# A Fourier mixing layer followed by a low-rank and channel mixer: late loads folded by quarters, u summed in PSUM, and a split last store

## The chip, the cores and the metric

The kernel runs on one core of a Trainium2 chip. The core has TensorE (PE, matmuls into PSUM; PEld is its weight load), VectorE (DVE), ScalarE (ACT), GpSimd (POOL) and SyncE (SP, which here only starts DMAs). Each has a queue of its own that it works off in order, and they wait for one another by semaphores. The metric is the device time of one execution in microseconds; of several executions the median is given.

## The reference

For each of 8 batches, `x` is a matrix of 3136 rows (sequence) and 256 columns. The first layer takes the real part of a two-dimensional Fourier transform. The second adds a low-rank mix along the sequence and then a two-layer channel mix with a residual:

```python
X = np.fft.fft(np.fft.fft(x, axis=1), axis=2).real
h = X.transpose(0, 2, 1) @ U @ V          # U: 3136 x 32, V: 32 x 3136
u = X + h.transpose(0, 2, 1)
out = u + np.maximum(u @ w_ch1, 0.0) @ w_ch2   # 256 -> 1024 -> 256
```

## The kernel before

**Transform.** The real part of the transform is symmetric, so only half of the rows (1568 per batch) is computed directly and the others are obtained as mirror images. Rows of `x` are loaded in four quarters q = 0..3, in two tiles: `xf` by GpSimd's gathers (`load_f`, line 69, one quarter each) and `xr` by SP's plain DMAs (`load_r`, line 74, one or two quarters each). "EV" is the quarters 0 and 2, "OD" 1 and 3. VectorE folds them: `along_d` (line 415) subtracts or adds columns and their mirror images into the bf16 tiles `EOF_` and `EOR_`; `alone` (line 422, on GpSimd) copies the two columns that have no partner; `mirror` (430) folds two quarters into `EOS`; `half` and `fourth` (434, 443) make `GE`, `GO` and `GC` of that. TensorE then multiplies these with tables of sines and cosines that ScalarE made at the start (`seq` at 539, `even_rows` at 595). ScalarE copies the first half of each product into `ev`, VectorE forms `eh` (`apart`) and joins the parts into the tiles `A` and `B` (`join`, `mirrored`). A second, short transform along the channels, `chan` (650) and, for the first rows of batch 0, `first_rows` (683), multiplies `A` and `B` with `MC` and `MSN` (or `MSX`) and leaves S and T, the two halves of the 256 channels for all 1568 rows. Calls of `filler` issue matmuls whose results are not used.

**Mixer.** The 8 x 1568 rows are worked off in 25 chunks of 512 columns, the last of 256. `front` (738) makes u of a chunk: TensorE multiplies V by the low-rank table `TA`, and VectorE adds S or T to it. It is done once for the rows themselves (hf = 0) and once for their mirrors (hf = 1). `direct` (798) is the first channel product for hf = 0, with ReLU on ScalarE; `mirrors` (814) corrects the same PSUM banks with WD and `uo`, which is S minus T, for hf = 1. `second_product` (855) is the second channel product. For most chunks u is also transposed by a DMA into `ut`, and VectorE adds that to the product (lines 882, 883), GpSimd adding a correction to one or two columns (887). For chunk 0 there is no `ut`: TensorE adds u by a matmul with a unit matrix `EM`, and ScalarE copies the sum (878). `store` (848) sends the output of a chunk to memory.

**Order.** Up to line 1131 the order of each engine's queue is the order of the source lines, written out by hand; from there on a planner orders the steps, with matmuls and folds kept in program order, and `put` and `turn` spread the work for the next batch over the chunks by due times. In the part written by hand stand, in this order: the loads; the sine tables; the folds of OD of `xr` and EV of `xf`, then those of EV of `xr` and OD of `xf` (lines 982 to 1010); on GpSimd between them the loads of V, W1 and W2 (992 to 995), the first gathers of batch 1 (1000) and the memsets of one row of `MSN` (1002); a copy of it to `MSX` on ScalarE (1021); the products of batch 0 (1026 to 1060); `lowrank`, which makes `TA`; `first_rows(0, 0)`, `hidden_0` and `front(0, 0)`; then `direct(0, 0)` and `chan(0, 2, ...)`.

PSUM banks are handed out in turn by tag: "dft" has two, "p1" four, "p2" two.

Of the kernel before, what the change touches and what calls it, by code (L numbers as in the profile page):

```python
# [16 lines left out]
P = 128  # L17
# [14 lines left out]
def kernel(  # L32
# [105 lines left out]
    load_r(x, xr, 0, 1, 2, D)  # L138
    r3()
    f0()  # L140
    load_r(x, xr, 0, 0, 2, D)
    iota(jv[:], [[1, KP]], 0, 1)
    for q in (0, 2):
        load_f(x, xf, 0, q, D)
# [277 lines left out]
    def alone(qs, src, dst, eng=None):  # L422

        (eng or nc.gpsimd.tensor_copy)(dst[:, qs, :, 128:257:128], src[:, qs, :, 0:129:128])
# [258 lines left out]
    def first_rows(b, at, tag):  # L683

        d = ST[b]
        n = 256 if at == 0 else 136
        for h in range(2):
            pt = psum.tile([P, 2, 256], FP32, tag=tag, name="psf", bufs=BUFS[tag])
            for c, lo in enumerate((at, 785 + at)):
                mm(pt[:, c, :n], MC[:, h * P:(h + 1) * P], d["A"][:, lo:lo + n], start=True, stop=False)  # L690
                mm(pt[:, c, :n], MSN[:, h * P:(h + 1) * P], d["B"][:, lo:lo + n], start=False, stop=True)
            to = strip(d["ST"[h]][:], 2 * at, [[1, 2], [2, n]])
            if h == 1:
                nc.vector.tensor_copy(to, pt[:, :, :n])
            else:
                nc.scalar.copy(to, pt[:, :, :n])

    def transposed(b, spare):

# [145 lines left out]

    out_f = out.rearrange("b n d -> (b n) d")

    def store(c, hf):

        o = CK[c]["o", hf]  # L850
        for row, p, np_, t, nt in blocks(c, hf):
            nc.sync.dma_start(out=bass.AP(out.tensor, out.offset + row * D, [[D, np_], [P * D, nt], [1, D]]),
                              in_=o[p:p + np_, t:t + nt, :])

    def second_product(c, hf, t0, w=2, rows=P, between=None):

        k = CK[c]
        h, ut = k["h", hf], k.get(("ut", hf))
        if t0 == 0:
            k["o", hf] = cp.tile([P, CH // P, D], FP32, tag="o", name="o", bufs=2)  # L860
        p2 = psum.tile([P, 2, D], FP32, tag="p2", name="p2", bufs=2)
        o = k["o", hf][:rows]
        for t in range(w):
            if t and between:
                between()
            at = (t0 + t) * P
            for j in range(JT):
                mm(p2[:rows, t, :], h[j // 4][:, j % 4, at:at + rows], W2[:, j, :],
                   start=(j == 0), stop=(j == JT - 1))
            if ut is None:  # L870
                parts = ((0, 1, P + 1), (1, P + 1, D), (1, 0, 1)) if hf else ((0, 0, P), (1, P, D))
                for s_, lo, hi in parts:
                    src = EM[:, P:P + 1] if hi == 1 else EM[:, lo:hi]
                    mm(p2[:rows, t, lo:hi], k["u", hf][:, s_, at:at + rows], src,
                       start=False, stop=True, skip_group_check=True)
        ts = slice(t0, t0 + w)
        if ut is None:
            nc.scalar.copy(o[:, ts, :], p2[:rows, :w, :])
            return
        tT = slice(CH // P + t0, CH // P + t0 + w)  # L880
        p2 = p2[:rows]
        nc.vector.tensor_tensor(o[:, ts, 0:P], p2[:, :w, 0:P], ut[:rows, ts, 0:P], op=AL.add)  # L882
        nc.vector.tensor_tensor(o[:, ts, P:D], p2[:, :w, P:D],  # L883
                                strip(ut[:rows], (CH // P + t0 + 1) * P, [[P, w], [-1, P]]), op=AL.add)
        fx = k["fx", hf]
        cols = slice(0, P + 1, P) if hf else slice(P, P + 1)
        nc.gpsimd.tensor_tensor(o[:, ts, cols], o[:, ts, cols], fx[:rows, ts, 1 - hf:], op=AL.add)  # L887
# [100 lines left out]
    msr = MSN[0:1].rearrange("p (l two) -> p l two", two=2)  # L988
    MDT = [MSN, MC]

    alone(EV, xf, EOF_)
    nc.gpsimd.dma_start(out=VV[:R, 0:S], in_=moe_V)
    gather(w1t[:], moe_w_ch1, D, pint[:], H, 0)
    nc.gpsimd.dma_start(out=W1[:, 0, :], in_=moe_w_ch1[0:P, :])
    nc.gpsimd.dma_start(out=W2[:], in_=moe_w_ch2.rearrange("(j p) d -> p j d", p=P))
    alone(EV, xr, EOR_)
    alone(OD, xf, EOF_)
    for part in range(2):
        along_d(EV, xf, EOF_, part)
    for q in (0, 2):  # L1000
# [3 lines left out]
    mirror(0, slice(0, 128), AL.subtract)  # L1004
    mirror(0, slice(128, 258), AL.add)
    for part in range(2):
        along_d(EV, xr, EOR_, part)
    along_d(OD, xf, EOF_, 0)
    mirror(1, slice(0, 128), AL.subtract)
    mirror(1, slice(256, 258), AL.add)  # L1010
    fill = filler()
# [10 lines left out]
    msr = MSX[0:1].rearrange("p (l two) -> p l two", two=2)  # L1022
    nc.gpsimd.memset(msr[:, :, 0:1], -1.0)
    nc.gpsimd.memset(msr[:, :, 1:2], 1.0)
    fill(22)
    for cols in (slice(0, 128), slice(256, 258)):
        half(0, 1, cols)
    seq(0, 1, 0, 0, "dft", False)
# [35 lines left out]
    filler("p2", spare)(3)  # L1064
    transposed(0, spare)
    join(0, 1, 0, sin_odd, low=False)
    nc.vector.tensor_tensor(WD[:], W1[:, 1, :], W1[:, 0, :], op=AL.subtract)
# [12 lines left out]
    nc.vector.tensor_copy(VV[2 * R:, S:S + 1], VV[2 * R:, HALF:HALF + 1])  # L1080
# [54 lines left out]
    for c in range(1, NCH):  # L1135
# [16 lines left out]
        if c + 1 < NCH:  # L1152
# [39 lines left out]
```

## Time and profile before

| what | value |
|---|---|
| median of 3 executions | 445.69 us (445.62 to 453.18) |
| profiled execution | 445.72 us |
| its span | 443.9 us |
| TensorE busy | 426.4 us (96%), granted clock 0.999 |
| VectorE busy | 318.2 us (72%) |
| ScalarE busy | 292.2 us (66%) |
| GpSimd busy | 134.7 us (30%) |
| moved by DMA | 67.83 MB, 153 GB/s in the mean |

The span runs from the first to the last instruction that the profile records; the execution's own time contains it and a little before and after. Busy time counts what an engine executes, not what its queue spends on waiting. A row of an engine in order of time gives the start, the duration, the engine, the line, the operation with what it writes and reads, its shape and, in brackets, how long the engine sat idle before it and what ended that wait. Neighbouring instructions of one kind are merged (x8), and a pipelined instruction's duration can overlap the next one's start.

### The profile page before, as it was taken

How to read it: one execution, taken by the hardware profiler on the slowest of the kernel's cores; microseconds unless marked ns; L12 is line 12 of the kernel's file. 1: busy time of each engine (PE TensorE's matmuls, PEld its weight loads, DVE VectorE, ACT ScalarE, POOL GpSimd, SP SyncE). 2: the span in 40 equal slices, each digit the busy share in tenths (PEclk: the TensorE clock that was granted, in tenths of full speed). 3: DMA queues.
4: the chain of work that ended last, by engine and by line, in shares of the span. 5: the costliest groups of instructions: out<-in, count | busy, mean ns of one | idle time of the engine just before them, and what ended most of it. 6: DMA issues, size and time to landing. Idle time of an engine off the chain costs nothing.

```text
span 443.9 us, 9378 instructions
## 1 busy us (share of the span) xinstructions
PE 426.4 (96%) x3501; PEld 283.5 (64%) x3501; DVE 318.2 (72%) x660; ACT 292.2 (66%) x633; POOL 134.7 (30%) x338
## 2 busy tenths in 40 slices
PE   5999989999999999999999999999999999999995
PEld 2663666656666676667666666656666666666674
DVE  8898976996798778769768778579767454353442
ACT  7957765766666756766667657766667657765751
POOL 8971321361214344433054122241232000011111
PEclk9999999999999999999999999999999999999999
DMA  7997697498297766845787385775334323334452
GB/s 199 234 229 155 147 276 108 128 229 229 68 211 178 191 169 159 249 93 153 186 161 220 92 209 69 162 206 120 83 91 140 99 72 103 93 120 118 120 144 97
DMA packets 89135, 67.83 MB, mean 153 GB/s; under 512 B 55372, under 2 KB 82400, under 8 KB 89088
## 3 DMA queue, kind: packets, MB, share of 16 engines
q1 hardware_dynamic: 83320, 52.79, 49.8%
q0 software_dynamic: 5472, 14.36, 12.5%
q8 instruction: 27, 0.44, 0.4%
q14 instruction: 20, 0.16, 0.1%
q10 hardware_dynamic: 296, 0.07, 0.1%
HBM read 28.86 MB, written 25.69 MB: 123 GB/s over the span
## 4 chain that ended last, share of the span: by engine, by line
PE 74%; DVE 11%; ACT 5%; DMA 4%; issue 3%; SPq 1%; POOL 0%; ACTq 0%; POOLq 0%; DVEq 0%
PE p L457 57%; PE pt L457 9%; PE pst L457 3%; DMA xr<-in_x_dram 3%; ACT h L812 3%; PE ph L457 2%; DVE u L767 2%; DVE eof L452 2%; DVE eor L452 1%; DMA out_dram<-o 1%; DVE eos L452 1%; PE ptt L457 1%; ACT ev L610 1%; DVE ge L452 1%; ACT S L664 1%
## 5 line engine op out<-in xcount | busy, mean ns | idle before, releaser
L457 PE MATMUL p<-w,h 128*128 128x256 bf16 x1576 | 195.2, 273 | 0.0
L457 PEld LDWEIGHTS <-h 128*128 128x128 bf16 x1576 | 148.6, 98 | 38.7 <-issue 15.4
L828 ACT ACTIVATE h<-p 128x512 bf16<-128x512 f32 (+1 forms) x200 | 101.6, 594 | 82.8 <-PE p L457 80.7
L812 ACT ACTIVATE h<-p 128x512 bf16<-128x512 f32 (+1 forms) x200 | 101.7, 597 | 11.0 <-PE p L457 8.4
L457 PE MATMUL p<-u,w 128*128 128x512 bf16 (+1 forms) x400 | 93.4, 374 | 0.9 <-DVE u L767 0.9
L882 DVE TENSOR_TENSOR o<-p,ut 128x256 f32<-128x256 f32 x95 | 39.7, 418 | 62.4 <-PE p L457 43.8
L887 POOL TENSOR_TENSOR o<-o,fx 128x2 f32<-128x2 f32 (+1 forms) x95 | 38.1, 401 | 132.7 <-DVE o L883 78.5
L457 PEld LDWEIGHTS <-w 128*128 128x128 bf16 x512 | 41.6, 97 | 38.7 <-issue 2.8
L457 PE MATMUL p<-uo,wd 128*128 128x512 bf16 (+1 forms) x200 | 50.8, 375 | 0.2
L57 POOL DMA_INDIRECT xf<-in_x_dram,xidx x32 | 39.2, 1224 | 24.0 <-DVE eof L452 12.9
L767 DVE TENSOR_TENSOR u<-ph,T 128x512 bf16<-128x512 f32 (+8 forms) x64 | 35.0, 558 | 9.2 <-PE ph L457 7.3
L452 DVE TENSOR_TENSOR eor<-xr 99x1016 bf16<-99x1016 f32 x32 | 38.2, 1209 | 2.1 <-DMA xr<-in_x_dram 1.9
L883 DVE TENSOR_TENSOR o<-p,ut 128x256 f32<-128x256 f32 x95 | 39.1, 411 | 0.0
L452 DVE TENSOR_TENSOR eof<-xf 99x1016 bf16<-99x1016 f32 x32 | 38.2, 1205 | 0.0
L767 DVE TENSOR_TENSOR u<-ph,S 128x512 bf16<-128x512 f32 (+8 forms) x64 | 34.9, 557 | 0.9 <-PE ph L457 0.3
L785 POOL TENSOR_TENSOR fx<-ut 128x4 f32<-128x4 bf16 x48 | 13.9, 290 | 57.4 <-DMA ut<-u 57.3
L784 POOL TENSOR_TENSOR fx<-ut 128x4 f32<-128x4 bf16 x24 | 8.8, 366 | 65.6 <-DMA ut<-u 65.6
L457 PEld LDWEIGHTS <-wd 128*128 128x128 bf16 x200 | 19.4, 98 | 13.2 <-issue 0.4
L457 PE MATMUL pt<-te,gc 98*128 98x229 bf16 (+1 forms) x192 | 24.2, 260 | 2.4 <-DVE u L767 1.3
L457 PEld LDWEIGHTS <-gc 98*128 98x128 bf16 x216 | 19.2, 97 | 8.4 <-issue 4.4
L664 ACT CAST S<-pst 128x392 bf16<-128x392 f32 (+1 forms) x30 | 18.6, 620 | 6.6 <-PE pst L457 6.6
L664 ACT CAST T<-pst 128x392 bf16<-128x392 f32 (+1 forms) x28 | 17.2, 613 | 7.4 <-PE pst L457 6.5
(172 smaller groups left out, 463.0 us busy)
## 6 DMA issues: line engine op xcount, KB each, us to landing
out_dram<-o SPq DMA_DIRECT2D x33, 512.0 KB
xr<-in_x_dram SPq DMA_DIRECT2D x16, 784.0 KB
out_dram<-o SPq DMA_DIRECT2D x8, 384.0 KB
out_dram<-o SPq DMA_DIRECT2D x9, 256.0 KB
out_dram<-o SPq DMA_DIRECT2D x8, 128.0 KB
ut<-u SPq DMA_TRANSPOSE x48
vv<-vv SPq DMA_DIRECT2D x3, 196.0 KB
out_dram<-o SPq DMA_DIRECT2D x6, 96.0 KB
```

The lines of the kernel that those rows point to most:

```text
L57: nc.gpsimd.indirect_dma_start(out_, None, bass.AP(t.tensor, t.offset, [[w, rows], [1, w]]), bass.IndirectOffsetOnAxis(idx, 0), element_of ...
L452: ins = nc.vector.tensor_tensor(*a, **k)
L457: ins = nc.tensor.matmul(*a, **k)
L664: nc.scalar.copy(to, pt[:, :n])
L767: nc.vector.tensor_tensor(u[:, s, at:at + hi - lo], phs[s][:, at:at + hi - lo], src, op=AL.add)
L784: nc.gpsimd.tensor_tensor(fx[:, :, 0], ut[:, n:2 * n, 0], ut[:, 0:n, 0], op=AL.subtract)
L785: nc.gpsimd.tensor_tensor(fx[:, :, 1], ut[:, 0:n, 0] if hf else ut[:, n:2 * n, 0], ut[:, n + 1:2 * n + 1, 0], op=AL.subtract)
L812: nc.scalar.activation(k["h", 0][q][:, j - 4 * q, :w], p1[:, :w], AF.Relu)
L828: nc.scalar.activation(k["h", 1][q][:, g, :w], k["p1"][g][:, :w][:, ::-1], AF.Relu)
L882: nc.vector.tensor_tensor(o[:, ts, 0:P], p2[:, :w, 0:P], ut[:rows, ts, 0:P], op=AL.add)
L883: nc.vector.tensor_tensor(o[:, ts, P:D], p2[:, :w, P:D], strip(ut[:rows], (CH // P + t0 + 1) * P, [[P, w], [-1, P]]), op=AL.add)
L887: nc.gpsimd.tensor_tensor(o[:, ts, cols], o[:, ts, cols], fx[:rows, ts, 1 - hf:], op=AL.add)
```

## The change

Four things are changed.

1. The quarters 0 and 2 of `xr` of batch 0 are loaded by two DMAs instead of one. `alone` and `along_d` for these quarters of `xr` and for the quarters 1 and 3 of `xf` are called for one quarter at a time, in the order xr 0, xf 1, xr 2, xf 3. Two of the four `alone` casts move on GpSimd ahead of loads of the weights. One run of unused matmuls has 15 instead of 22.
2. The first u (`front(0, 0)`) is replaced by `first_u`: TensorE sums the channel transform and the low-rank part in one PSUM bank for each half of the channels, and ScalarE and VectorE copy one bank each. The computation of WD and `first_rows(0, 0)` come behind it, and both copies of `first_rows(0, 0)` are VectorE's.
3. The last 256 rows of the output are worked off as two tiles of 128, each with its own store.
4. For the second of these, u is added by TensorE with `EM`, and the columns are copied out in two parts, by ScalarE and by VectorE.

```diff
@@ loads
-    load_r(x, xr, 0, 0, 2, D)
+    for q in (0, 2):
+        load_r(x, xr, 0, q, 1, D)
@@ first_rows
-            if h == 1:
+            if h == 1 or at == 0:
                 nc.vector.tensor_copy(to, pt[:, :, :n])
             else:
                 nc.scalar.copy(to, pt[:, :, :n])
+    def first_u():
+
+        d = ST[0]
+        u = cp.tile([P, 2 * CH // P, P], BF16, tag="u0", name="u0", bufs=2)
+        u = CK.setdefault(0, {})["u", 0] = u[:].rearrange("p (s t) m -> p s (t m)", s=2)
+        pts = [psum.tile([P, 2, 256], FP32, tag="dft", name="psu", bufs=BUFS["dft"]) for h in range(2)]
+        for h, pt in enumerate(pts):
+            for c in range(2):
+                lo = 785 * c
+                mm(pt[:, c, :], MC[:, h * P:(h + 1) * P], d["A"][:, lo:lo + 256], start=(c == 0), stop=False,
+                   skip_group_check=True)
+                mm(pt[:, c, :], MSN[:, h * P:(h + 1) * P], d["B"][:, lo:lo + 256], start=False, stop=True,
+                   skip_group_check=True)
+        for c in range(2):
+            for h, pt in enumerate(pts):
+                rows = slice(h * R, (h + 1) * R)
+                mm(pt[:, c, :], TA[0][rows, h * P:(h + 1) * P], VV[rows, c:CH:2], start=False, stop=True,
+                   skip_group_check=True)
+        for h, pt in enumerate(pts):
+            to = strip(u[:, h], 0, [[1, 2], [2, 256]])
+            if h:
+                nc.vector.tensor_copy(to, pt[:])
+            else:
+                nc.scalar.copy(to, pt[:])
@@ store: only = one tile of 128 rows
+            if only is not None:
+                if not t <= only < t + nt:
+                    continue
+                row, t, nt = row + (only - t) * P, only, 1
@@ second_product(..., end=False)
-        h, ut = k["h", hf], k.get(("ut", hf))
+        h, ut = k["h", hf], None if end else k.get(("ut", hf))
+        if end:
+            nc.scalar.copy(o[:, ts, 0:P], p2[:rows, :w, 0:P])
+            nc.vector.tensor_copy(o[:, ts, P:D], p2[:rows, :w, P:D])
+            return
@@ folds of batch 0
     alone(EV, xf, EOF_)
+    alone(one(0), xr, EOR_)
     nc.gpsimd.dma_start(out=VV[:R, 0:S], in_=moe_V)
     gather(w1t[:], moe_w_ch1, D, pint[:], H, 0)
+    alone(one(1), xf, EOF_)
     nc.gpsimd.dma_start(out=W1[:, 0, :], in_=moe_w_ch1[0:P, :])
     nc.gpsimd.dma_start(out=W2[:], in_=moe_w_ch2.rearrange("(j p) d -> p j d", p=P))
-    alone(EV, xr, EOR_)
-    alone(OD, xf, EOF_)
+    alone(one(2), xr, EOR_)
+    alone(one(3), xf, EOF_)
...
     for part in range(2):
-        along_d(EV, xr, EOR_, part)
-    along_d(OD, xf, EOF_, 0)
+        along_d(one(0), xr, EOR_, part)
+    along_d(one(1), xf, EOF_, 0)
+    for part in range(2):
+        along_d(one(2), xr, EOR_, part)
+    along_d(one(3), xf, EOF_, 0)
...
-    fill(22)
+    fill(15)
@@ first chunk
     join(0, 1, 0, sin_odd, low=False)
-    nc.vector.tensor_tensor(WD[:], W1[:, 1, :], W1[:, 0, :], op=AL.subtract)
-    nc.gpsimd.memset(WD[0:1], 0.0)
-    first_rows(0, 0, "dft")
-    hidden_0(0, spare)
     setup.close()
     cp = ctx.enter_context(tc.tile_pool(name="cp", bufs=2))
-    front(0, 0)
+    first_u()
+    hidden_0(0, spare)
     load_r(x, xr, 1, 0, 2, D)
     load_0f(1)
     mirrored(0, 0, sin_even)
     join(0, 1, 1, cos_odd, low=False)
+    nc.vector.tensor_tensor(WD[:], W1[:, 1, :], W1[:, 0, :], op=AL.subtract)
+    nc.gpsimd.memset(WD[0:1], 0.0)
+    first_rows(0, 0, "dft")
     odd_part(0)
     mirrored(0, 1, cos_even)
@@ the end
-    second_product(NCH - 1, 1, 0)
-    store(NCH - 1, 1)
+    second_product(NCH - 1, 1, 0, 1)
+    store(NCH - 1, 1, 0)
+    second_product(NCH - 1, 1, 1, 1, end=True)
+    store(NCH - 1, 1, 1)
```

More of the change, by code (lines that the diff above doesn't have):

```diff
@@ L846, with store, second_product @@
     out_f = out.rearrange("b n d -> (b n) d")
-    def store(c, hf):
+    def store(c, hf, only=None):
         o = CK[c]["o", hf]
         for row, p, np_, t, nt in blocks(c, hf):
+            if only is not None:
+                if not t <= only < t + nt:
+                    continue
+                row, t, nt = row + (only - t) * P, only, 1
             nc.sync.dma_start(out=bass.AP(out.tensor, out.offset + row * D, [[D, np_], [P * D, nt], [1, D]]),
                               in_=o[p:p + np_, t:t + nt, :])
-    def second_product(c, hf, t0, w=2, rows=P, between=None):
+    def second_product(c, hf, t0, w=2, rows=P, between=None, end=False):
         k = CK[c]
-        h, ut = k["h", hf], k.get(("ut", hf))
+        h, ut = k["h", hf], None if end else k.get(("ut", hf))
         if t0 == 0:
@@ L989, with one @@
     MDT = [MSN, MC]
+    def one(q):
+        return slice(q, q + 1)
     alone(EV, xf, EOF_)
+    alone(one(0), xr, EOR_)
     nc.gpsimd.dma_start(out=VV[:R, 0:S], in_=moe_V)
     gather(w1t[:], moe_w_ch1, D, pint[:], H, 0)
+    alone(one(1), xf, EOF_)
     nc.gpsimd.dma_start(out=W1[:, 0, :], in_=moe_w_ch1[0:P, :])
     nc.gpsimd.dma_start(out=W2[:], in_=moe_w_ch2.rearrange("(j p) d -> p j d", p=P))
-    alone(EV, xr, EOR_)
-    alone(OD, xf, EOF_)
+    alone(one(2), xr, EOR_)
+    alone(one(3), xf, EOF_)
     for part in range(2):
```

## The prediction

> **What bounds the kernel now.** I read the page first, then the chain that ended last, then each engine in order of time for the first 45 us and the last 10, the two places that the change touches.
>
> ```profile
> span 443.9 us, 9378 instructions
> PE 426.4 (96%) x3501; PEld 283.5 (64%) x3501; DVE 318.2 (72%) x660; ACT 292.2 (66%) x633; POOL 134.7 (30%) x338
> ```
>
> TensorE is busy for all but 17.5 us. From about 64 us to 439 it hardly waits, so a microsecond won at the start should arrive at the end, and nothing between moves. The chain shows what the start hangs on:
>
> ```profile
> 4.86 14.03 DMA xr<-in_x_dram
> ...
> 36.96 0.83 PE pst L457 x4
> ```
>
> The load of two quarters of `xr` takes 14.03 us and lands at 18.9; VectorE stands idle for it and then works almost without a gap up to the `pst` matmuls of the first `chan` at 36.96. That instant, call it C, sets the rest: the mirrored first product and its ScalarE evictions follow it in a fixed order.
>
> ```profile
> 18.92 2.36 DVE L452 TENSOR_TENSOR eor<-xr 99x1016 bf16<-99x1016 f32 x2 [1.91 <-DMA xr<-in_x_dram]
> 21.20 1.22 DVE L452 TENSOR_TENSOR eof<-xf 99x1016 bf16<-99x1016 f32 x1
> 22.45 0.78 DVE L452 TENSOR_TENSOR eos<-eor,eof 99x1024 bf16<-99x1024 bf16 x2
> ```
>
> VectorE idles 1.91 us, folds three slabs (3.5 us) and reaches `eos` at 22.45. This is what the folding by quarters attacks. The question is who else stands at that place:
>
> ```profile
> 24.01 0.84 PE L457 MATMUL pt<-ts,go 98*128 98x196 bf16 x8 [0.37 <-DVE go L452]
> ...
> 27.52 0.85 PE L457 MATMUL pt<-te,gc 98*128 98x197 bf16 x8
> ...
> 31.94 0.27 PE L457 MATMUL psf<-A,mc 128*128 128x256 bf16 x1
> ```
>
> ```profile
> 25.14 0.40 ACT L1021 COPY msx<-msn 128x256 bf16<-128x256 bf16 x1 [3.22 <-POOL msn L1003]
> 25.45 0.48 ACT L554 COPY ev<-pt 128x392 f32<-128x392 f32 x1
> 25.83 1.05 ACT L1030 CAST w<-w1t 128x1024 bf16<-128x1024 f32 x1
> 26.91 0.49 ACT L610 COPY ev<-pt 128x393 f32<-128x393 f32 x1
> ```
>
> ```profile
> 18.95 1.30 POOL L424 CAST eor<-xr 99x16 bf16<-99x16 f32 x1 [0.64 <-DMA xr<-in_x_dram]
> 20.15 1.24 POOL L424 CAST eof<-xf 99x16 bf16<-99x16 f32 x1
> 21.53 1.78 POOL L57 DMA_INDIRECT xf<-in_x_dram,xidx  x1
> 23.61 1.10 POOL L57 DMA_INDIRECT xf<-in_x_dram,xidx  x1 [0.30 <-issue]
> 24.72 0.24 POOL L1002 MEMSET msn<- 1x128 bf16 x1
> 24.87 0.23 POOL L1003 MEMSET msn<- 1x128 bf16 x1
> ```
>
> The matmuls at 27.52 continue in the bank that the `ev` copy of 26.91 empties until 27.40. That copy stands on ScalarE behind the `msx` copy, which waited 3.22 us for GpSimd's `msn` memsets, and these are queued behind two casts and two gathers. So two paths reach 27.5 within 0.1 us of each other: VectorE's folds, and GpSimd, then ScalarE. Shortening the first alone wins nothing there.
>
> **The change part by part.**
>
> *Late half of x by quarters.* One load becomes two of half the size, each issued by SP; the second is issued about 0.5 us later, into a queue that is busy anyway. I take the first quarter to land before 17.0 (bounds: halfway through the 14.03 us, at 11.9, and 18.9) and the second at 18.9 as before. Three folds (2.36 + 1.22 less overlap, 3.5 us) become six of half the length. A row of 1016 elements takes 1.2 us, so a half takes 0.6 to 0.7 and the six some 0.2 us more in all. Three of them fit into the idle 1.91 us. VectorE then reaches `eos` at 18.9 + 3 x 0.61 = 20.7, 1.7 us early. The shorter fill (15 for 22) takes seven of 0.17 us off TensorE ahead of that, 1.2 us, which lets it start at about 22.5 and reach the 27.52 place at 26.0 if nothing else holds it.
>
> *GpSimd's queue.* Two casts become four. The first now stands ahead of the loads of V and W1, the second ahead of those of W1 and W2; whoever waits for these weights does so after 25 us. Each cast in the rows ends just behind a VectorE fold that ran when it began: the pair of folds from 18.92 ends at 20.1 and 21.3, the casts at 20.25 and 21.39. With folds of half the length I price a cast at 0.4 to 0.7, and the first, beside a full one, at 1.2; the 0.64 us wait for `xr` goes, since the weights' issues now fall past that landing. The four end at about 20.9 to 21.7, against 21.39. The first gather took 1.78 us beside a 1.22 us fold; beside shorter folds 1.1 to 1.4. So the `msn` memsets end earlier by g = 0.2 to 1.0 us; I take 0.7, and this, not the 1.7, is what passes 27.5. The `first_u` matmuls then begin at 31.94 - (g + 0.2); the 0.2 are small waits for VectorE that go. They cannot begin before 26.0 + 4.3 = 30.3.
>
> The Trainium skill, "SBUF — State Buffer", section "SBUF: two separate sides", says that VectorE and GpSimd hold a shared port pair as an exclusive lock for a whole instruction. By that, shorter folds free the casts sooner; but it also says that descriptors for DMAs issued by GpSimd cannot be written while VectorE runs an operation that takes both ports, and the weights' issues, which lay in VectorE's idle stretch, would now meet VectorE's work. Whether a fold is such an operation no row shows; if it is, that speaks against the change, at the second rival's place.
>
> *First u summed by TensorE, and VectorE's list up to C.*
>
> ```profile
> 32.31 0.68 DVE L1067 TENSOR_TENSOR wd<-w 128x1024 bf16<-128x1024 bf16 x1
> 33.02 0.73 DVE L694 CAST T<-psf 128x512 bf16<-128x512 f32 x1
> ...
> 35.04 0.59 DVE L629 SCALAR_TENSOR_TENSOR B<-ev,pt 128x392 bf16<-128x392 f32 x1
> 35.53 0.54 DVE L582 TENSOR_TENSOR A<-eh,pt 128x392 bf16<-128x392 f32 x1
> 35.99 0.41 DVE L792 TENSOR_TENSOR uo<-S,T 128x512 bf16<-128x512 bf16 x1
> 36.32 0.59 DVE L629 SCALAR_TENSOR_TENSOR A<-ev,pt 128x392 bf16<-128x392 f32 x1
> ```
>
> ```profile
> 39.02 0.39 PE L457 MATMUL p<-dv,qf 32*128 32x512 bf16 x4
> 39.25 0.38 PE L457 MATMUL ph<-vv,ta 32*128 32x512 bf16 x2
> ```
>
> Before, 5.02 us lie between the first `psf` matmul (31.94) and C (36.96). After, `first_u` puts eight matmuls of 256 columns (the eight of 197 columns start about 0.083 us apart, so 0.11 each, 0.88) and four of 32 rows there. Four 32-row matmuls of 512 columns occupied 0.23 us, so these take 0.2 to 0.25; they read VV with a step of two, which no row shows, and at half rate it would be 0.25 more. Nothing below zero is in it: they are added work. That is 1.13 us, and 0.2 until VectorE sees the end. VectorE's own copy of u stands at the head of its list, so it waits there, with nothing to do, and then has: u copy 0.66, `mirrored` 0.49, `join` 0.46, WD 0.68, two `first_rows` casts of 0.66 (one was ScalarE's), `uo` 0.33, `mirrored` 0.64 up to C. The sum is 4.58, and 5.91 from the start of `first_u` to C: 0.89 us longer. The direct product itself starts earlier (u no longer goes through two casts and two additions), but TensorE's next work is the `chan` at C, and there it stops. The `first_rows` matmuls, 0.88 us more on TensorE, lie in the shadow of the u copies and cost nothing; without that cover they would cost their 0.88.
>
> Start: gain g + 0.2 - 0.89 = 0.0 us for g = 0.7, between -0.5 and +0.3 for the bounds of g, and +0.75 at the most (first matmul at 30.3).
>
> *The end.*
>
> ```profile
> 439.02 0.42 DVE L882 TENSOR_TENSOR o<-p,ut 128x256 f32<-128x256 f32 x1 [1.44 <-PE p L457]
> 439.37 0.42 DVE L883 TENSOR_TENSOR o<-p,ut 128x256 f32<-128x256 f32 x1
> 439.91 0.21 POOL L887 TENSOR_TENSOR o<-o,fx 128x4 f32<-128x4 f32 x1 [2.07 <-issue]
> 440.15 0.38 SPq L852 DMA_DIRECT2D out_dram<-o  x1
> ```
>
> ```profile
> 441.25:441.50 0.25, 0.00 (x0) 0.00 (x0) 0.00 (x0) 0.00 (x0) 0.00 (x0) 1.00 1.09 389
> ```
>
> The last store of 256 KB moves at 389 GB/s, 0.67 us; half of it needs 0.34, and the first half is on its way about a microsecond earlier, with its issue of 0.38 clear of the second. That is 0.33 gained. Ahead of it the second tile gains three small matmuls (0.16 at 0.05 each) and loses two additions and GpSimd's correction. Its two copies read one PSUM bank from two engines:
>
> ```profile
> 65.55 0.33 ACT L616 CAST tab<-pt 128x128 bf16<-128x128 f32 x1
> ...
> 65.91 0.59 DVE L629 SCALAR_TENSOR_TENSOR A<-ev,pt 128x392 bf16<-128x392 f32 x1 [2.49 <-ACT tab L616]
> ```
>
> `tab` is nothing that line 629 uses; they share only the bank `pt`, and VectorE waited 2.49 us for it. So I take the copies one behind the other: TensorE's end just ahead of 439.02, plus 0.16, then 0.3 (ScalarE, 128x128) and 0.3 (VectorE; bounds 0.2 and 0.42), the issue at about 439.8 instead of 440.15. Gain 0.35 + 0.33 = 0.7; side by side it would be 1.0; and 0.3 if a copy cost 0.42 and the first store delayed the second.
>
> **The sum** against the profiled execution: 445.72 us with a span of 443.9, so 1.8 us lie outside it and stay. 445.72 - 0.0 - 0.7 = 445.0. The median shown, 445.69, is the same within 0.03.
>
> **Rivals.**
>
> *The folds' gain passes through.* If the shorter VectorE stretch also lets GpSimd run ahead so that TensorE is held by nothing at 27.5, and `first_u` hides VectorE's list better than I count, start 0.75 to 1.7 and end 1.0: 443.0 to 444.0. For it: 1.91 us of idle VectorE really go. Against: the 3.22 us wait for `msn`.
>
> *GpSimd becomes the bound and it is slower than before.* If each of the four casts takes the 1.24 us of the rows, they end at 18.3 + 5.0 = 23.3 instead of 21.39; even 21.39 plus an unchanged 3.7 us to the memsets (g = 0) costs 0.7 at C, as much as the end wins, so it decides from there: memsets later than 25.1 means slower than before. Price at 23.3: 1.9 + 0.7 lost, 0.7 won, 447.6; nearer the middle 446.5. For it: every cast beside a fold in the rows took 1.2 to 1.3. Against: those folds were twice as long.
>
> *The second quarter lands later.* By a fixed cost of each transfer the split would delay it. At 2 us later `eos` comes at 22.7, the start loses about 1.0 and the time is 446.0. For it nothing in the rows, against it that the queue is full throughout. The Trainium skill, "DMA: Bandwidth & Descriptors", section "Rules for kernel authors", advises to join small transfers; it gives a fixed cost of some 2.0 us each, and no row here separates that cost.
>
> *The end does not do what it says*: extra matmuls, serial copies and a second issue eat the smaller store, gain 0: 445.7.
>
> **How the numbers follow.** Forecast 445.0 (444.5 to 445.5): 0.52. Gain passes through: 0.15. GpSimd later: 0.20. Late quarter: 0.05. End worth nothing: 0.08. The range 443.6 to 446.9 leaves out about half of the first rival and half of the second. 2% is 8.9 us, about what a measurement of this kernel can tell from no change; no case reaches it, so within 2% has 0.98 and each side 0.01.
>
> **What will show it.** VectorE's idle stretch before `xr` gone and `eos` near 20.7; the `msn` memsets ending between 24.1 and 24.9; the `msx` copy still released by them; TensorE waiting about a microsecond for VectorE ahead of the first `pst`; the last VectorE copy behind ScalarE's; the end of the span 3.4 us behind the last issue, instead of 443.9 - 440.15 = 3.75. I am wrong if `msn` ends after 25.1, if the first `pst` comes before 36.2 or after 37.5, or if the planned middle, which is ordered anew from there, puts in waits that it did not have.

## The result and the profile after

| | before | after |
|---|---|---|
| median | 445.62 us (21 executions) | 444.36 us (21 executions) |
| ratio of the times | | 0.9963, 95% interval 0.9946 to 0.998 |
| span of the profiled execution | 443.9 us | 442.5 us |
| first `pst` matmul (C) | 36.96 us | 36.60 us |
| start of the last `p<-uo,wd` | 433.43 us | 433.09 us |

The medians take all executions, while the ratio and its interval, here and below, are of the fast ones alone, so the ratio need not be the quotient of the medians. The change gains 1.26 us in the medians and 1.4 us between the two spans, 0.3%. Of the 1.4 us, 0.34 are there at the start and stay to the last `p<-uo,wd` matmuls; the other 1.06 come behind these. First the page of after, its span and the busy times (the three dots in this and the other excerpts stand for lines left out):

```profile
span 442.5 us, 9402 instructions
...
PE 426.2 (96%) x3507; PEld 284.4 (64%) x3507; DVE 318.5 (72%) x664; ACT 292.5 (66%) x634; POOL 129.4 (29%) x340
```

TensorE is busy for as long as before (426.2 us, 426.4 before); what went is idle time. VectorE of after in order of time, the folds and then the list from the copy of u to C:

```profile
17.28 1.27 DVE L453 TENSOR_TENSOR eor<-xr 99x508 bf16<-99x508 f32 x2
...
19.07 1.27 DVE L453 TENSOR_TENSOR eor<-xr 99x508 bf16<-99x508 f32 x2
...
20.98 0.78 DVE L453 TENSOR_TENSOR eos<-eor,eof 99x1024 bf16<-99x1024 bf16 x2
...
32.08 0.73 DVE L720 CAST u<-psu 128x512 bf16<-128x512 f32 x1 [1.16 <-POOL em L283]
...
35.96 0.59 DVE L630 SCALAR_TENSOR_TENSOR A<-ev,pt 128x392 bf16<-128x392 f32 x1
```

No fold waits for a load any more, and `eos` starts at 20.98 instead of 22.45. Further down VectorE stands idle for 1.16 us ahead of its copy of u and then works without a gap up to C. The row names GpSimd's `em` as what ended that wait; the `psu` matmuls end at the same time, for ScalarE's copy of the other half, which they release, begins at 32.04, so `em` costs 0.04 us at the most. GpSimd and ScalarE of after:

```profile
15.72 0.50 POOL L425 CAST eor<-xr 99x8 bf16<-99x8 f32 x1 [0.60 <-DMA xr<-in_x_dram]
...
18.29 0.34 POOL L425 CAST eof<-xf 99x8 bf16<-99x8 f32 x1
18.56 0.59 POOL L1033 DMA_DIRECT2D w<-in_moe_w_ch_dram  x1
19.14 0.96 POOL L1034 DMA_DIRECT2D w<-in_moe_w_ch_dram  x1
...
20.34 0.67 POOL L425 CAST eof<-xf 99x8 bf16<-99x8 f32 x1
21.18 1.39 POOL L57 DMA_INDIRECT xf<-in_x_dram,xidx  x1 [0.17 <-POOL eof L425]
...
24.08 0.24 POOL L1042 MEMSET msn<- 1x128 bf16 x1
```

```profile
24.35 0.40 ACT L1063 COPY msx<-msn 128x256 bf16<-128x256 bf16 x1 [2.41 <-POOL msn L1042]
```

The first quarter has landed by 15.7. The memsets end at 24.3, 0.8 us earlier than before, and the `msx` copy is still released by them. TensorE of after, from the place that stood at 27.52 to the first `pst`:

```profile
26.53 0.85 PE L458 MATMUL pt<-te,gc 98*128 98x197 bf16 x8
...
30.59 0.27 PE L458 MATMUL psu<-A,mc 128*128 128x256 bf16 x1
...
31.56 0.40 PE L458 MATMUL psu<-vv,ta 32*128 32x256 bf16 x4
31.89 0.60 PE L458 MATMUL spare<-w,td 128*128 128x512 bf16 x2
...
36.60 0.34 PE L458 MATMUL pst<-A,mc 128*128 128x393 bf16 x1 [1.02 <-DVE A L630]
```

`first_u` starts 1.35 us before the `psf` matmuls of before (31.94). From there to C lie 6.01 us, where 5.02 were, and 1.02 of them are a wait for VectorE. So 0.36 is left. At the end, TensorE of before and of after, then the queues of after:

```profile
433.43 0.60 PE L457 MATMUL p<-uo,wd 128*128 128x256 bf16 x4
```

```profile
433.09 0.60 PE L458 MATMUL p<-uo,wd 128*128 128x256 bf16 x4
```

```profile
438.80 0.27 ACT L908 COPY o<-p 128x128 f32<-128x128 f32 x1 [3.58 <-PE p L458]
```

```profile
439.09 0.29 DVE L909 COPY o<-p 128x128 f32<-128x128 f32 x1 [0.79 <-ACT o L908]
```

```profile
439.41 0.34 SPq L882 DMA_DIRECT2D out_dram<-o  x1
```

The last issue comes 6.32 us behind the start of these `p<-uo,wd` matmuls, where before it came 6.72 behind (440.15): 0.40 gained. The last bytes of both kernels, in slices of 0.1 us (the last two columns are the DMA share and GB/s), before and then after:

```profile
441.80:441.90 0.10, 0.00 (x0) 0.00 (x0) 0.00 (x0) 0.00 (x0) 0.00 (x0) 1.00 0.06 10
```

```profile
440.60:440.70 0.10, 0.00 (x0) 0.00 (x0) 0.00 (x0) 0.00 (x0) 0.00 (x0) 1.00 0.47 144
```

Data end at the edge of these slices, at about 441.85 and 440.7, 1.7 and 1.3 us behind the last issue: 0.4 gained by the smaller store. From there to the end of the span it is 2.05 us before and 1.8 after: another 0.25. The three make up the 1.06.

### The profile page after: what moved, and what is told of

Same layout as the page of the kernel before. It is cut to its first block, busy times and chain, and to the rows that moved or that the text cites. A ratio compares the mean times of both kernels' runs of the same rounds, so it can differ in the third digit from the quotient of the medians.

```text
span 442.5 us, 9402 instructions
## 1 busy us (share of the span) xinstructions
PE 426.2 (96%) x3507; PEld 284.4 (64%) x3507; DVE 318.5 (72%) x664; ACT 292.5 (66%) x634; POOL 129.4 (29%) x340
## 4 chain that ended last, share of the span: by engine, by line
PE 74%; DVE 9%; ACT 6%; DMA 4%; issue 3%; POOL 2%; SPq 1%; ACTq 0%; DVEq 0%; POOLq 0%
PE p L458 58%; PE pt L458 8%; PE pst L458 3%; ACT h L838 3%; DMA xr<-in_x_dram 2%; PE ph L458 2%; DVE u L793 2%; DVE eof L453 2%; DMA out_dram<-o 1%; PE ptt L458 1%; ACT ev L611 1%; DVE eos L453 1%; POOL xf L57 1%; DVE ge L453 1%; DVE eor L453 1%
## 5 line engine op out<-in xcount | busy, mean ns | idle before, releaser
L916 DVE TENSOR_TENSOR o<-p,ut 128x256 f32<-128x256 f32 (+1 forms) x95 | 39.5, 416 | 61.4 <-PE p L458 42.5
L793 DVE TENSOR_TENSOR u<-ph,T 128x512 bf16<-128x512 f32 (+23 forms) x63 | 34.3, 556 | 9.2 <-PE ph L458 7.3
L917 DVE TENSOR_TENSOR o<-p,ut 128x256 f32<-128x256 f32 (+1 forms) x95 | 38.9, 409 | 0.0
L453 DVE TENSOR_TENSOR eof<-xf 99x1016 bf16<-99x1016 f32 (+1 forms) x33 | 38.3, 1172 | 0.3 <-issue 0.3
L453 DVE TENSOR_TENSOR eor<-xr 99x1016 bf16<-99x1016 f32 (+1 forms) x34 | 38.3, 1143 | 0.1
L793 DVE TENSOR_TENSOR u<-ph,S 128x512 bf16<-128x512 f32 (+23 forms) x63 | 34.2, 554 | 0.8 <-PE ph L458 0.3
L458 PE MATMUL pst<-A,mc 128*128 128x392 bf16 (+1 forms) x60 | 19.8, 330 | 2.8 <-DVE A L630 1.0
```

Of the source, the lines that this page charges most:

```text
L453: ins = nc.vector.tensor_tensor(*a, **k)
L458: ins = nc.tensor.matmul(*a, **k)
L793: nc.vector.tensor_tensor(u[:, s, at:at + hi - lo], phs[s][:, at:at + hi - lo], src, op=AL.add)
L917: nc.vector.tensor_tensor(o[:, ts, P:D], p2[:, :w, P:D], strip(ut[:rows], (CH // P + t0 + 1) * P, [[P, w], [-1, P]]), op=AL.add)
```

## The experiments

All spans, and all times inside an execution, are of one profiled execution; the medians are of 6 to 12 executions (21 of after, 21 to 35 of before in each of four sets). "At 42" and "at 288" are the differences to before at the weight loads of the `p<-uo,wd` matmuls that begin at 42 and 288 us in before, "at 433" the same for the last ones; "end" is what the span then gains (+) behind these. The table:

| kernel | C | at 42 | at 288 | at 433 | end | span | median |
|---|---|---|---|---|---|---|---|
| before | 36.96 | 0 | 0 | 0 | 0 | 443.9 | 445.38 to 446.73 |
| after | 36.60 | -0.34 | -0.50 | -0.33 | +1.07 | 442.5 | 444.36 |
| after, again | 36.12 | -0.82 | -1.07 | +5.07 | +1.07 | 447.9 | 444.44 |
| new end alone | 36.06 | -0.90 | -1.07 | -1.02 | +0.98 | 441.9 | 444.90 |
| quarters alone | 35.72 | -1.24 | -1.36 | -0.40 | 0.00 | 443.5 | 445.44 |
| first u alone | 37.85 | +0.90 | +0.50 | +3.69 | 0.00 | 447.6 | 449.31 |
| memsets first | 36.87 | -0.08 | -0.22 | +0.14 | +1.14 | 442.9 | 444.55 |
| list moved | 35.88 | -1.07 | -1.30 | +2.13 | +1.13 | 444.9 | 446.54 |
| no first u | 35.18 | -1.78 | -1.88 | -1.04 | +1.06 | 441.8 | 444.03 |
| no first u, memsets first | 35.49 | -1.47 | -1.56 | -0.89 | +1.11 | 441.9 | 444.39 |
| six matmuls more | 38.95 | +1.99 | +1.60 | +3.94 | -0.06 | 447.9 | 449.81 |
| store in parts | 36.69 | -0.26 | +0.58 | +1.22 | +0.32 | 444.8 | 445.49 |
| one copy | 35.98 | -0.96 | -1.12 | -0.83 | +1.07 | 442.0 | 443.97 |
| gathers moved | 37.20 | +0.25 | +4.25 | +7.57 | -0.03 | 451.5 | 454.40 |

The theory: the start gives about what GpSimd's queue gives, less the cost of first u; the end gives the rest; nothing between moves. The rivals: the gain of the folds passes through whole; or a stretch near 290 us, where the kernel with first u alone lost 3.2 us, decides by the time at which a kernel arrives there.

### The parts alone

The new end on the kernel before (the lines that use it; the two helpers are changed as in the change):

```diff
-    second_product(NCH - 1, 1, 0)
-    store(NCH - 1, 1)
+    second_product(NCH - 1, 1, 0, 1)
+    store(NCH - 1, 1, 0)
+    second_product(NCH - 1, 1, 1, 1, end=True)
+    store(NCH - 1, 1, 1)
```

> The kernel before with the two changes of the end alone (two stores, the residual of the last tile by TensorE and two copies). Theory, that about 1.05 us of the 1.4 us between the two spans (443.9 and 442.5) are won here: the last issue 0.40 us earlier than 440.15, the store itself 0.39 us shorter, and some 0.27 us less from its last byte to the end of the span; span 442.8 to 442.9. Rival, that only what I forecast belongs to the end (0.35 and 0.33) and the rest to the start: span 443.2.

Ratio 0.9982 (0.9944 to 1.0019). Behind the last mark it gains 0.98 us, as the whole change does: the end adds up by itself. Its C is 0.90 us earlier than in before, though no instruction ahead of C is changed. Here the load of `xr` landed 0.98 us earlier: the rows of VectorE of this kernel and of the kernel with first u alone, against 18.92 in before:

```profile
17.94 2.35 DVE L452 TENSOR_TENSOR eor<-xr 99x1016 bf16<-99x1016 f32 x2 [1.24 <-DMA xr<-in_x_dram]
```

```profile
16.93 2.39 DVE L452 TENSOR_TENSOR eor<-xr 99x1016 bf16<-99x1016 f32 x2 [0.21 <-DMA xr<-in_x_dram]
```

In the six profiles that have this load it lands between 16.9 and 19.9 us (19.91 in the kernel with six matmuls more). It is not the only thing that C hangs on: with first u alone it landed 2 us before that of before, and `psu` began only 0.11 us before 31.94, since TensorE itself, which had no gap from 20.45 to 24.26, came to the first product later (24.26, where before it was 24.01). A single C can't be read to better than a microsecond, so the distance from the first `psf` or `psu` to C is the surer measure.

The load and the folds by quarters, with the fill of 15, on the kernel before (the folds and casts as in the change):

```diff
-    load_r(x, xr, 0, 0, 2, D)
+    for q in (0, 2):
+        load_r(x, xr, 0, q, 1, D)
...
-    fill(22)
+    fill(15)
```

> The kernel before with the late half of x loaded and folded by quarters and the shorter fill alone; the first u is made as before. Theory, that the folds and GpSimd's queue bring the first rows' matmuls from 31.94 to about 30.6 and that the first u summed by TensorE then gives back about 0.9 us of it: here the way from the first rows to the first pst stays 5.0 us, pst at 35.6 instead of 36.60, span 442.5. Rival, that the new first u is what brings the gain: pst at 36.6 or later, span 443.5 or more.

Ratio 1.0006 (0.9977 to 1.0035): nothing in the time, although C comes at 35.72. Of the 1.36 us that it is early at 288, 0.96 are gone at the next such mark (297), across a wait for the transposed `qf` that before does not have:

```profile
289.09 0.33 PE L458 MATMUL p<-dv,qf 32*128 32x352 bf16 x4 [0.68 <-DMA qf<-qt]
```

First u on the kernel before (with WD and `first_rows` behind it, as in the change):

```diff
-    front(0, 0)
+    first_u()
```

> The kernel before with the first u summed by TensorE, WD and the first rows behind it, alone. Theory: its matmuls begin at 31.9 as the first rows did, the way to pst is 6.0 us instead of 5.0, pst at 37.9 instead of 36.96, span 444.9. Rival, that the earlier first u brings a gain of its own: pst at or before 36.9, span 443.9 or less.

Ratio 1.0071 (1.0039 to 1.0102). From the first `psu` (31.83) to C (37.85) it is 6.02 us, where before and the two kernels above have 5.02, 5.02 and 5.01: first u costs 1.0 us at C. It loses 3.2 us more behind 288 us, again across that wait:

```profile
292.49 0.33 PE L457 MATMUL p<-dv,qf 32*128 32x352 bf16 x4 [2.23 <-DMA qf<-qt]
```

### What holds TensorE ahead of C

The two `msn` memsets ahead of the two gathers, in the changed kernel:

```diff
+    nc.gpsimd.memset(msr[:, :, 0:1], 1.0)
+    nc.gpsimd.memset(msr[:, :, 1:2], -1.0)
     for q in (0, 2):
         load_f(x, xf, 1, q, D)
-    nc.gpsimd.memset(msr[:, :, 0:1], 1.0)
-    nc.gpsimd.memset(msr[:, :, 1:2], -1.0)
```

> The changed kernel with GpSimd's two msn memsets moved ahead of the two gathers of batch 1. Theory, that the msx copy on ScalarE is what holds TensorE back after 26.2: the msx copy starts at about 22.0 instead of 24.35, TensorE goes on at 26.25 instead of 26.53, the first u and pst come 0.3 us earlier (30.3 and 36.3), span 442.2. Rival, that VectorE or the loads hold it anyway: nothing moves by more than 0.1 us.

Ratio 1.0003 (0.9971 to 1.0035); medians 444.55 and, of before, 445.65. ScalarE and TensorE of this kernel:

```profile
21.85 0.40 ACT L1063 COPY msx<-msn 128x256 bf16<-128x256 bf16 x1
```

```profile
26.43 0.85 PE L458 MATMUL pt<-te,gc 98*128 98x197 bf16 x8
```

The `msx` copy waits for nothing now and is done 2.5 us earlier, and TensorE passes the place at 26.43 instead of 26.53, with VectorE's `eos` 0.36 us later than in after (21.34). So GpSimd's queue held TensorE by some tenths at the most; the folds stand right behind it. In the changed kernel both paths end within some tenths of each other, where before it was 0.1. C did not come at 36.3 but at 36.87, later by 0.27 than in after, as `eos` is; the gain of 0.3 is not seen.

Two operations of VectorE ahead of `first_u`, in the changed kernel:

```diff
+    mirrored(0, 0, sin_even)
+    join(0, 1, 1, cos_odd, low=False)
     first_u()
...
-    mirrored(0, 0, sin_even)
-    join(0, 1, 1, cos_odd, low=False)
```

> The changed kernel with two operations of VectorE (the mirrored sums of the even sines, 0.49 us, and the join of the odd cosines, 0.46 us) moved from behind first_u to ahead of it; nothing else differs. Theory: in the changed kernel VectorE stands idle for 1.16 us in front of its copy of u and then works through its list up to the first pst matmul, so these 0.95 us fit into the idle time: from the start of the first psu matmul to the first pst matmul 5.1 us instead of 6.0, the first pst at about 35.7, the span 0.9 us shorter (about 441.6), unless a later wait takes it back. Rival: the list is not what holds pst (TensorE, the evictions of the direct product or a landing is): 6.0 us between them as before, span 442.5. Third: the shift changes the stall near 290 us, and the span moves by less or more than C does.

Ratio 0.9984 (0.9946 to 1.0023). TensorE of this kernel:

```profile
30.65 0.27 PE L458 MATMUL psu<-A,mc 128*128 128x256 bf16 x1
...
35.88 0.34 PE L458 MATMUL pst<-A,mc 128*128 128x393 bf16 x1 [0.24 <-DVE A L630]
```

5.23 us from `psu` to C instead of 6.01, with 0.95 us of VectorE's work taken out from between, and the wait ahead of `pst` falls from 1.02 to 0.24: it is VectorE's list that holds C, as the theory has it. But the span is 444.9 instead of 441.6: behind 288 us the kernel loses 3.43 us, and its median (446.54) is no better than that of before on the same chip (446.73).

The changed kernel without first u (`front(0, 0)` and the order of before in its place):

> The kernel before with the load and folds by quarters, the fill of 15 and the new end, without the first u by TensorE. Theory: the parts add up: 5.0 us between the first psf matmul and the first pst matmul, pst at about 35.7 (35.72 in the kernel with the quarters alone), end 1.0 us shorter than before, so a span of 441.6 if the stall near 290 us stays as it is before, and 442.6 if it takes 0.96 us as in the kernel with the quarters alone. Against the changed kernel 0.9 us faster or the same. Rival: quarters and first u need each other (the fold's gain shows only with it): pst at 36.6 or later, span 442.9 or more.

Ratio 0.9957 (0.9919 to 0.9995). 5.02 us from `psf` (30.16) to C, which is at 35.18: the earliest of all. Quarters and end work without first u. Of 1.88 us at 288 us, 0.84 are given back behind it. The same with the memsets first, beside the changed kernel once more on one chip:

> The changed kernel without the first u by TensorE (so quarters, fill of 15 and the new end), with the two msn memsets ahead of the two gathers of the second batch. Theory: without first u the first pst matmul comes 1.0 us earlier than in the changed kernel at the same landing; the memsets give 0.1 more at most, since TensorE's evictions and VectorE stand at that place by then. Median 443.5, 0.7 to 1.0 us below the changed kernel on the same chip. Rival: the stall near 290 us takes 0.9 us of it back, as it took 0.84 in the kernel without first u and 0.17 in the changed one: the two are the same within 0.2 us.

> The changed kernel, run beside the next two on one chip. Expected as before: first pst matmul near 36.6 or up to 0.7 us earlier, as the landing of the late rows of x moves between executions; span 442 to 443, median 444.2 to 444.6, 0.3 to 0.4% below before.

Ratios 0.9991 (0.9966 to 1.0015) and 1.0012 (0.9983 to 1.0041); medians 444.39 and 444.44. Without first u, C was 0.63 us earlier in the one profile of each (35.49 and 36.12), and the medians differ by 0.05 us. That is what the rival of the first of these expectations says; the intervals are wide enough that the 0.7 us of the theory are not excluded. Of the 12 executions of the changed kernel here, 8 took 443.6 to 445.5 us and 4 took 447.9 to 450.0, which lifts its ratio over that of the first set; the profiled one is among the four and loses 6.14 us between the marks at 288 and 297, while from mark to mark on both sides of that its distance to before changes by less than 0.2 us. So the loss lies at one place and is no general slowness.

### The loss near 290 us

The kernel before with a later start:

```diff
-    filler("p2", spare)(3)
+    filler("p2", spare)(9)
```

> The kernel before with nine filling matmuls instead of three ahead of the transposed rank part, so that the first psf matmul and all behind it come up to 1.0 us later; no part of the change is in it. Theory: the stall near 290 us goes by the moment at which the middle arrives there, not by what the edits do: with C about 0.9 us later, as in the kernel with first u alone, it takes some 2 to 3 us more there, and the span is 447 to 448. Rival: the stall of that kernel came from first u itself (other buffers, other order): here the shift of 0.9 us arrives at the end and the span is about 444.8. Third: the six matmuls are hidden, C does not move and nothing is learnt.

Ratio 1.0087 (1.0057 to 1.0117), all 12 executions between 448.8 and 451.9. It was 1.60 us late at 288 us and lost 2.34 more, with nothing of the change in it. So the loss isn't first u's. (Of the 1.99 us at C, 1.0 are the six matmuls and about as much is the landing of `xr`, 19.91.) But the arrival doesn't decide it alone either: every execution of the two late kernels took 448.2 us or more, yet the kernel with the list moved came 1.30 us early and lost 3.43, and the changed kernel came 0.50 early and lost 0.17, and 1.07 early and lost 6.14. These last two are executions of one program, so their rows can be laid side by side. First SP's queue in after, then in after again:

```profile
259.42 1.66 SPq L807 DMA_TRANSPOSE ut<-u  x1
...
268.42 4.61 SPq L807 DMA_TRANSPOSE ut<-u  x1
...
283.61 1.44 SPq L746 DMA_TRANSPOSE qf<-qt  x1
```

```profile
258.85 4.02 SPq L807 DMA_TRANSPOSE ut<-u  x1
...
270.31 4.73 SPq L807 DMA_TRANSPOSE ut<-u  x1
...
285.89 1.98 SPq L746 DMA_TRANSPOSE qf<-qt  x1
```

Up to 258.85 the second runs 0.57 us ahead. There the issue of one transpose takes 4.02 us instead of 1.66, and GpSimd's corrections `fx`, which wait for the transposed u, begin 0.57 us later than in the first. By the rows, what makes microseconds of that is the next step, the second `fx`. GpSimd of after, then GpSimd and VectorE of after again:

```profile
266.88 0.20 POOL L811 TENSOR_TENSOR fx<-ut 128x4 f32<-128x4 bf16 x1
```

```profile
267.45 1.90 POOL L811 TENSOR_TENSOR fx<-ut 128x4 f32<-128x4 bf16 x1
```

```profile
268.09 1.20 DVE L453 TENSOR_TENSOR eof<-xf 99x1016 bf16<-99x1016 f32 x1
```

The same `fx` takes 1.90 us instead of 0.20 and ends 0.06 us behind VectorE's fold. All five profiles that lose over 2 us (this one, first u alone, list moved, six matmuls more, gathers moved) have such an `fx` here, of 1.14 to 1.90 us, ending 0.06 to 0.07 us behind that fold; in the other nine it takes 0.20 to 0.43 us and is over before the fold begins. No run was made to test this step by itself. SP's stores between the transposes wait for GpSimd, so the next two transposes come 1.89 and 2.28 us later than in the first. TensorE and VectorE of after again:

```profile
293.08 0.48 PE L458 MATMUL p<-dv,qf 32*128 32x352 bf16 x4 [4.39 <-DMA qf<-qt]
```

```profile
291.25 0.42 DVE L916 TENSOR_TENSOR o<-p,ut 128x256 f32<-128x256 f32 x1 [8.14 <-DMA out_dram<-o]
```

TensorE has nothing to do until `qf` lands, and VectorE stands 8.14 us for a store that is to free the buffer of `o`. So a late transpose at 259 us reaches TensorE at 289 us over SP, GpSimd and SP again. In the three kernels with quarters and without first u the same stretch takes back 0.67 to 0.96 us of the early start: in the kernel without first u a transposed u is late on GpSimd near 277 us, and TensorE then waits 0.52 us for `qf`. The two kernels with C at 36.06 and 35.98 lose only 0.04 and 0.3 there. GpSimd of after, then GpSimd and TensorE of that kernel:

```profile
276.75 0.20 POOL L811 TENSOR_TENSOR fx<-ut 128x4 f32<-128x4 bf16 x1 [3.93 <-DMA ut<-u]
```

```profile
276.78 0.76 POOL L786 TENSOR_TENSOR fx<-ut 128x4 f32<-128x4 bf16 x1 [5.33 <-DMA ut<-u]
```

```profile
288.40 0.33 PE L458 MATMUL p<-dv,qf 32*128 32x352 bf16 x4 [0.52 <-DMA qf<-qt]
```

`fx` begins 0.03 us later than in after, though TensorE stands 1.4 us earlier at that time. Why the issue of one transpose takes 4.02 us and that of another 1.66 no row shows: that stays open. It isn't needed for the loss, either: with first u alone and with six matmuls more it took 1.89 and 2.05 us, and there the transpose itself was issued late (261.43 and 262.53, before 259.92).

A try to break the chain: the delayed kernel (six matmuls more) with the next batch's gathers ahead of the folds of `xr`; this is the line that places them:

```diff
-            yield lambda qf=qf: along_d(qf, xf, EOF_, 1)
+            yield lambda qf=qf, nm=nm: (along_d(qf, xf, EOF_, 1), gathers(b + 1, nm))
```

> The delayed kernel (before, with nine filling matmuls instead of three), which lost 2.3 us near 290 us in its profile, with the gathers of the next batch issued on GpSimd ahead of the folds of xr instead of behind them, in all batches. Theory: the stall begins near 255 us, where a transposed u lands some tenths of a microsecond too late, the GpSimd operations behind it and the gather then start inside VectorE's folds and take 1.8 to 2.5 us instead of 1.0, and SP's stores and transposes fall behind; with the gathers elsewhere the stall goes or shrinks: 1.6 us behind before at 288 us and also at the end, span 445.5. Rival: the gathers are not the cause: 3.9 us behind before at the end, span 447.8. Third: the new place meets other waits, and a new stall appears at another place; then the profile has to show which wait it is.

Ratio 1.0211 (1.0186 to 1.0236). The loss near 290 us stays (3.3 us), so the gathers' place isn't its cause, or not the only one; and the third case comes true, 4.4 us are lost at a new place, between the marks at 132 and 140 us of before. TensorE of this kernel:

```profile
138.31 0.39 PE L457 MATMUL p<-u,w 128*128 128x512 bf16 x1 [2.65 <-DVE u L771]
...
295.98 0.33 PE L457 MATMUL p<-dv,qf 32*128 32x352 bf16 x4 [1.97 <-DMA qf<-qt]
```

### The end, term by term

The store in two parts, the second tile's residual still by VectorE and GpSimd; against the kernel with the new end alone it differs in:

```diff
-    second_product(NCH - 1, 1, 1, 1, end=True)
+    second_product(NCH - 1, 1, 1, 1)
```

> The kernel before whose last rows are computed and stored tile by tile in two parts, the second tile's residual still added by VectorE and GpSimd from the transposed u. Theory: the gain of the new end, 0.98 to 1.14 us from the last weight loads to the end of the span, has three terms: about 0.4 for the residual by TensorE, 0.39 for the halved store, 0.27 for its shorter completion. Here the last two remain and VectorE's two additions are of half the width: 0.7 us gained at the end. Rival: the gain is all in the residual, since GpSimd's correction and the two additions stood in the way: 0.4 us or less here.

Ratio 0.9986 (0.9949 to 1.0022). TensorE and SP's queue of this kernel, and the slice in which its data end:

```profile
434.65 0.60 PE L457 MATMUL p<-uo,wd 128*128 128x256 bf16 x4
```

```profile
440.97 0.34 SPq L856 DMA_DIRECT2D out_dram<-o  x1
```

```profile
442.20:442.30 0.10, 0.00 (x0) 0.00 (x0) 0.00 (x0) 0.00 (x0) 0.00 (x0) 1.00 0.19 52
```

The issue is 6.32 us behind the mark and the last data 7.65: as in after (6.32 and 7.6). The residual by TensorE and two copies therefore wins nothing over two additions and a correction on a tile of half the width; all that moves the data is the split. The span gains only 0.32, since it ends 2.5 us behind the data instead of 1.8. (The delay of this kernel in the table has nothing to do with its end: 0.95 us are lost between the marks at 68 and 81 us, where VectorE waits 4.88 us for a store, and 0.63 behind 288.)

One copy instead of two, in the changed kernel:

```diff
-            nc.scalar.copy(o[:, ts, 0:P], p2[:rows, :w, 0:P])
-            nc.vector.tensor_copy(o[:, ts, P:D], p2[:rows, :w, P:D])
+            nc.scalar.copy(o[:, ts, :], p2[:rows, :w, :])
```

> The changed kernel whose last tile is copied by one ScalarE copy of 256 columns instead of a ScalarE and a VectorE copy of 128 each. Theory: the two copies of the changed kernel run one behind the other on one PSUM bank (0.27 and 0.29 us, issue at 0.61 us behind the start of the first); one copy of 256 columns by ScalarE takes about 0.35 to 0.45, so the last issue comes 0.1 to 0.2 us earlier behind the last matmul. Rival: the copies only seem serial, and one copy of twice the width is later by 0.1 or more.

Ratio 0.9981 (0.9953 to 1.0008), median 443.97, beside 444.44 of the changed kernel on that chip. ScalarE of this kernel:

```profile
438.30 0.37 ACT L908 COPY o<-p 128x256 f32<-128x256 f32 x1 [3.58 <-PE p L458]
```

One copy of 256 columns takes 0.37 us where the two took 0.58 one behind the other, so the data end 0.2 us earlier behind the last matmuls. Behind the data, the span ends 2.0 us later instead of 1.8, and so keeps nothing of it (1.07 as in after). This kernel and the one without first u have the lowest medians of all, 443.97 and 444.03; neither can be told from the changed kernel's 444.36 and 444.44, as their intervals overlap.

## Why the prediction was right, and where it was not

**The whole.** 445.0 was predicted and 444.36 measured, inside the range and 0.14 below the forecast's own stretch of 444.5 to 445.5; in the profiled execution 443.9 - 442.5 = 1.4 us instead of 0.7. Both terms were too small by 0.36.

**GpSimd passes the start, VectorE doesn't.** g was put at 0.7 and came out at 0.8. The first cast took 0.50 us, where 1.2 had been counted, and the two shown behind it 0.34 and 0.67 (priced at 0.4 to 0.7); `msx` is still released by `msn`. `eos` came at 20.98 for 20.7, since VectorE had work until 17.28. That both paths stand within some tenths of the same place is shown by the run with the memsets first. The second rival, GpSimd slower than before, is out: the memsets end before 25.1 in every run with quarters. The Trainium skill, "SBUF — State Buffer", section "SBUF: two separate sides", speaks of DMA descriptors that GpSimd cannot write while VectorE runs an operation in a two-port mode. The two W issues took 0.59 and 0.96 us beside folds (0.64 and 1.01 before), so they are no case of it.

**First u.** 0.89 us were counted between its start and C, and 0.99 measured in after, 1.0 in the run alone. VectorE's list holds C, as the run with the list moved shows; the missing tenth is the four small matmuls, 0.33 us to the next instruction instead of 0.2 to 0.25. What failed is the other side of the sum, the "small waits" of 0.2 ahead of it: the start came 1.35 us earlier, not 0.9. With g at 0.8 these waits are 0.55: TensorE passes the place of 27.52 at 26.53, 0.99 earlier, and gains 0.36 more from there to `first_u` (4.42 us before, 4.06 after). The gain of 0.36 us at C is itself of one pair of profiles, and the landing of `xr` moves C by about as much as the whole change. Several profiles together say the same: C stands at 36.06 to 36.96 in three with the old load (before, new end, store in parts), at 35.18 to 35.72 in three with quarters and without first u, and at 35.98 to 36.60 in three with both (after twice, one copy). So quarters gain about 1.1 us in the mean, first u takes some 0.8 of that, and 0.3 is left.

**The end.** The three terms: the issue 0.40 for 0.35, the smaller store 0.4 for 0.33, and 0.25 behind the last data for nothing. The copies do run one behind the other, as predicted (whether for the bank that they share or for the tile `o` that both write, no run separates), and the end of the span stands 3.1 us behind the last issue, not 3.4. That the gain of 0.35 at the issue belonged to TensorE's residual and the two copies is wrong: the store in parts gets the same issue without them.

**"Nothing between moves."** This is the step that failed, though the profiles of before and after hide it. Between the marks at 288 and 297 us nearly every kernel changes its distance to before, through the chain that begins near 258: the early ones give back 0.04 to 0.96 us, five profiles lose 2.3 to 6.1. In the first profile of the changed kernel it was 0.17, and the forecast depended on that. The prediction named waits in the planned middle as a sign of being wrong, and gave them no price; the second profile of the changed kernel has them.

## What to carry to other kernels

A microsecond won at the start is worth what the tightest chain behind it lets through. Look for the DMA that lands just in time for its reader, and see how it stood in several executions, before counting a gain as one that arrives. Splitting the last store is the sure gain here (about 0.8 us to the last data, in every kernel that has it), and who adds the residual ahead of it makes no difference. A queue that works in order stops at an operation that waits, though ready work stands behind it: VectorE stood 1.16 us ahead of its copy of u, and with two ready operations moved ahead of that the way to C fell from 6.01 to 5.23 us. Without first u it is 5.02, though no median shows that 1.0 us (444.03 beside 444.36).

## What the runs showed of the hardware

- One load of two quarters, issued at 4.86 to 4.87 us in every case, let VectorE go on between 16.93 and 19.91 us in six profiles.
- The issue of the same transposing DMA took 1.66 and 4.02 us on SP's queue in two executions of one program, and the second execution lost 6 us 30 us later.
- A GpSimd operation on 128x4 elements took 0.20 us when it was over before a VectorE fold began, and 1.90 us when it was not; it then ended 0.06 us behind the fold.
- From the last data to the end of the span it was 2.05 to 2.1 us in five profiles with one last store of 256 KB, 1.7 to 1.85 in seven with the whole new end, but 2.0 with one copy and 2.5 with the store in parts alone, which also end with 128 KB. So it isn't the size of the store alone; one packet of 8 KB in the queue for instructions falls into that time in before and in the store in parts, and what it does wasn't tried.
- Two copies of 128 columns from one PSUM bank, by ScalarE and VectorE, took 0.58 us in a row, and one ScalarE copy of 256 columns 0.37.
